# Attention, expert layer and MLP on one core: the first loads in another order, and the value tiles with places of their own in the plan

## The chip, the cores and the metric

The kernel runs on one core of one Trainium2 chip. The metric is the device time of one execution in microseconds (us). The core has a matrix engine (PE, with its weight loads shown as PEld), a vector engine (DVE), a scalar engine (ACT), GpSimd (POOL) and SyncE (SP), which here only issues DMA transfers. Each engine runs its own instructions in order. They meet through semaphores.

## The reference, cut to what matters

```python
# attention: q, k, v (4, 8, 576, 64), s (4, 8, 576)
scores = scale * q @ k.T                       # per batch and head
cum    = cumsum(maximum(s, 0))                 # the "decay sums"
bias   = -(cum[:, :, :, None] - cum[:, :, None, :])
scores = where(causal, -1e9, scores + minimum(bias, 0))
attn   = softmax(scores);  x = attn @ v        # (2304, 512)
# expert layer: each token goes to the best of 8 experts, 512 -> 1024 -> 512
# MLP: 512 -> 2048 -> 512 with h * clip(h + 3, 0, 6) / 6
```

## The kernel before

All products of fp32 data are made of fp16 halves: a number is split into `hi` and `lo`, and three products are summed. The change lies in the attention stage.

Attention has four batches. A batch has five units (128 query rows each, the last one 64), a unit four pairs of heads, so there are 80 pairs. For one pair, PE makes the scores (`S`, L575), DVE adds the decay sums and takes the minimum (`A`, L588), ACT takes the exponential (`E`, L594), PE transposes the result (`T`, L603), ACT and DVE split it (`CD`, L624 and L625), and PE multiplies it with `v` (`V`, L658). A loop over `n` issues step S of pair n+1, A and E of pair n, T and CD of pair n-1, and V of pair n-2; functions put into slot n by `at_slot` or `at_time` follow. `at_time` counts in a plan in which a pair of the five units costs 1.0, 1.5, 2.2, 2.9 and 2.3 (`price`). A scheduler then orders each engine's instructions by a simulated time line, except where `issue_after` ties one instruction behind another.

Four kinds of side work run beside the pairs:

- `load` brings a chunk of 256 rows of q and k (the last chunk has 64). `prep` turns it: POOL lines it up (`xs`), PE transposes (L490), ACT, DVE or POOL split it into `qT` and `kT`.
- `load_v` brings 128 rows of `v` into `v32`, which has two buffers. The `v_part` function makes the halves: ACT writes `hi` (L514), POOL scales (L445) and subtracts (L516). In the kernel before, `v_part` is part of `prep`, and its steps follow the turns of its chunk.
- The decay sums are scanned by DVE for all batches at once (`run`), written to memory (`cum_d`, L407) and read back, repeated over 128 partitions, into the tile `cp` of a batch (`load_cum`, L414). For the first 128 columns of four heads, `first_cum` builds `cp` with PE (L426) and a copy by ACT (L431).
- `fold_cum` copies parts of `cp` for the unit of 64 rows (POOL, L445, 64x576). For the fourth batch these are eight copies into a tile of their own.

From the third batch's fourth unit on, the first expert's weights are loaded (`wf`) and split on POOL (L249, L251, L246) and ACT (L250). POOL also scatters the tokens of a batch (`tok_d`, L804) and gathers rows for the first expert pass (`xg`, L204). Then follow ten expert passes (PE lines L1130 and L1241) and the MLP (L1267 and L1350).

## Time and profile before

| | |
|---|---|
| runs | 875.09, 870.36, 871.22 us; median 871.22 |
| profiled execution | 872.09 us, its span 870.3 us |
| busy over the span | PE 91%, PEld 76%, DVE 72%, ACT 53%, POOL 34% |
| mean granted clock of PE | 0.963 of 2.4 GHz |
| attention stage | from the start to about 275 us |

The span goes from the first to the last instruction of the profiled execution. A row of the chain of waits names what the end of the kernel, followed backwards, waited for at each time; "SPq" is SP's issue of a transfer. In a row of a time line, the brackets at the end give how long the engine was idle before the instruction and what released it.

### The profile page before, as it was taken

Reading aid. Unit: us, or ns where it says so; the run is one execution under the profiler, and the core shown is the slowest. Engines: PE = TensorE matmul, PEld = TensorE weight load, DVE = VectorE, ACT = ScalarE, POOL = GpSimd, SP = SyncE. Lnnn points to the kernel's source line nnn. Section 1 sums busy time; section 2 is a strip of 40 time slices with the busy share of each in tenths; the row PEclk is TensorE's granted clock in tenths of the full one; section 3 lists DMA queues with packets and bytes.
Section 4 is the critical chain, followed back from the end, with each engine's and each line's share of the span. In section 5 each row is a group of like instructions: output and inputs, shape, how many; then the busy total and the mean of one; then the engine's idle time right before and its main releaser. Section 6 shows DMA issues by size and latency. Waiting matters only on the chain.

```text
span 870.3 us, 21871 instructions
## 1 busy us (share of the span) xinstructions
PE 794.4 (91%) x8340; PEld 659.7 (76%) x8340; DVE 623.5 (72%) x1542; ACT 461.7 (53%) x854; POOL 296.4 (34%) x402
## 2 busy tenths in 40 slices
PE   5888788888888998899999999999999999999993
PEld 4567567666667897566778888888888888888882
DVE  4677777866767645789879569988677777777770
ACT  3677767867875433666656343554444344443440
POOL 2565663868984225044331100000022022211232
PEclk8799999999999999999999999999999999999997
DMA  7957245243613678988887355654444545444420
GB/s 165 262 130 214 70 89 180 51 96 101 178 47 79 171 209 219 321 304 273 256 259 270 98 170 165 220 174 158 141 148 129 159 150 162 142 141 153 153 95 27
DMA packets 154327, 142.03 MB, mean 163 GB/s; under 512 B 68710, under 2 KB 122214, under 8 KB 153446
## 3 DMA queue, kind: packets, MB, share of 16 engines
q1 hardware_dynamic: 150422, 130.50, 50.2%
q0 software_dynamic: 3792, 10.06, 3.5%
q8 instruction: 67, 1.10, 0.5%
q14 instruction: 46, 0.38, 0.2%
HBM read 106.70 MB, written 28.54 MB: 155 GB/s over the span
## 4 chain that ended last, share of the span: by engine, by line
PE 48%; DMA 17%; DVE 10%; POOL 7%; ACT 5%; issue 5%; SPq 4%; another core or an unknown queue 1%; POOLq 0%; ACTq 0%; DVEq 0%
PE bank L1350 18%; PE py L1241 8%; PE bank L1267 8%; PE ph L1130 7%; DMA wf<-in_moe_w_dram 5%; DMA v<-in_v_dram 3%; PE pt L603 2%; PE sp L575 2%; PE o L658 2%; DVE wo L1110 2%; DMA t_d<-cl 2%; DMA xsT<-xg 1%; DMA t_d<-sets 1%; ACT pp L594 1%; SPq L215 1%
## 5 line engine op out<-in xcount | busy, mean ns | idle before, releaser
L1267 PE MATMUL bank<-x2T,wi 128*128 128x256 f16 x1728 | 193.5, 273 | 0.9 <-POOL x2T L1249 0.6
L1267 PEld LDWEIGHTS <-wi 128*128 128x128 f16 x1728 | 169.1, 98 | 21.0 <-issue 1.5
L1350 PE MATMUL bank<-wo,sets 128*128 128x256 f16 x1512 | 170.2, 273 | 1.2 <-DVE sets L1279 0.7
L1350 PEld LDWEIGHTS <-sets 128*128 128x128 f16 x1512 | 147.7, 98 | 19.0 <-DVE sets L1279 1.0
L1278 ACT ACTIVATE sets<-back 128x896 f16<-128x896 f32 x72 | 68.1, 950 | 91.9 <-PE bank L1350 74.7
L1130 PE MATMUL ph<-xsT,t 128*128 128x224 f16 (+7 forms) x960 | 109.6, 276 | 3.6 <-DVE hT L1135 3.6
L1241 PE MATMUL py<-hT,t 128*128 128x224 f16 (+7 forms) x960 | 108.4, 273 | 4.2 <-DVE hT L1135 2.3
L1361 POOL TENSOR_TENSOR u<-sa 128x256 f32<-128x256 f32 x9 | 9.3, 1035 | 296.4 <-ACT sa L1360 296.4
L1130 PEld LDWEIGHTS <-t 128*128 128x128 f16 x960 | 86.8, 99 | 24.1 <-issue 4.2
L1241 PEld LDWEIGHTS <-t 128*128 128x128 f16 x960 | 85.5, 98 | 25.7 <-issue 5.7
L1279 DVE SCALAR_TENSOR_TENSOR sets<-back,sets 128x896 f16<-128x896 f32 x72 | 80.2, 1119 | 22.1 <-ACT sets L1278 21.9
L625 DVE SCALAR_TENSOR_TENSOR lo<-pt,hi 128x256 f16<-128x256 f32 (+3 forms) x144 | 72.8, 519 | 28.5 <-ACT hi L624 27.4
L257 DVE SCALAR_TENSOR_TENSOR t<-wf,t 128x1024 f16<-128x1024 f32 x53 | 66.7, 1258 | 28.6 <-ACT t L254 27.9
L658 PE MATMUL o<-v,hi 128*128 128x65 f16 (+2 forms) x960 | 63.0, 201 | 24.9 <-ACT hi L624 17.9
L603 PE MATMUL pt<-idf,pp 128*128 128x128 f32 (+1 forms) x400 | 77.9, 310 | 7.5 <-DVE kT L499 1.9
L624 ACT ACTIVATE hi<-pt 128x256 f16<-128x256 f32 (+3 forms) x144 | 64.1, 460 | 35.4 <-PE pt L603 27.0
L594 ACT ACTIVATE pp<-ne,nm 128x128 f32<-128x128 f32 (+4 forms) x144 | 76.9, 580 | 0.6 <-DVE nm L588 0.6
L254 ACT ACTIVATE t<-wf 128x1024 f16<-128x1024 f32 x53 | 55.5, 1053 | 36.1 <-DMA wf<-in_moe_w_dram 36.1
L588 DVE CUSTOM_DVE_ANT_0 ne<-sp,cp 128x128 f32<-128x128 f32 (+4 forms) x144 | 61.2, 456 | 16.5 <-ACT pp L594 11.4
L658 PEld LDWEIGHTS <-hi 128*128 128x128 f16 (+2 forms) x960 | 47.9, 104 | 32.3 <-ACT hi L624 21.0
L603 PEld LDWEIGHTS pt<-idf,pp 128*128 128x128 f32 (+1 forms) x400 | 46.9, 152 | 17.5 <-issue 3.6
L1249 POOL TENSOR_TENSOR x2T<-y,x2T 128x360 f32 (+5 forms) x24 | 20.8, 871 | 111.1 <-ACT x2T L1248 97.4
(206 smaller groups left out, 1263.4 us busy)
## 6 DMA issues: line engine op xcount, KB each, us to landing
wf<-in_moe_w_dram SPq DMA_DIRECT2D x64, 512.0 KB
back<-t_d SPq DMA_DIRECT2D x144, 128.0 KB
wd<-in_moe_w_in_dram SPq DMA_DIRECT2D x16, 512.0 KB
wd<-in_moe_w_out_dram SPq DMA_DIRECT2D x16, 512.0 KB
cp<-cum_d SPq DMA_DIRECT2D x6, 1152.0 KB
t_d<-cl SPq DMA_DIRECT2D x24, 256.0 KB
t_d<-sets SPq DMA_DIRECT2D x24, 256.0 KB
t_d<-wo SPq DMA_DIRECT2D x24, 256.0 KB
```

The costliest lines, as they stand in the source:

```text
L257: stt(out=lo, in0=fv, scalar=sc, in1=hi, op0=ALU.mult, op1=ALU.subtract)
L594: mark["act"] = nc.scalar.activation(self.view(self.pp, e), self.view(self.ne, e), AF.Exp, bias=self.nm[:, e:e + 1], scale=-1.0).ins
L603: nc.tensor.transpose(self.pt[g][:m, x, :], src, idf)
L624: nc.scalar.activation(hi, pt, AF.Copy, scale=SP)
L625: stt(out=lo, in0=pt, scalar=SP, in1=hi, op0=ALU.mult, op1=ALU.subtract)
L658: mark["pe"] = nc.tensor.matmul(dst, a, x, start=first, stop=last).ins
L1130: mark["pe"] = nc.tensor.matmul(ph[:, :n], wt[c][:, a, cols], xT[:, KD * b_ + c, :n], start=(c == 0 and x == 0), stop=(c == KD - 1 and x = ...
L1241: nc.tensor.matmul(py[:, :rows], wt2[:, j_, f, cols], hT[i_][:, f, :rows], start=(f == 0 and x == 0), stop=(f == KF - 1 and x == 2),)
L1267: m = nc.tensor.matmul(dst, wi[:, a, kk, fs], x2[:, KD * b_ + kk], start=(kk == 0 and x == 0), stop=(kk == KD - 1 and x == 2),)
L1278: nc.scalar.activation(hi, t, AF.Copy, scale=SG)
L1279: stt(out=lo, in0=t, scalar=SG, in1=hi, op0=ALU.mult, op1=ALU.subtract)
L1350: m = nc.tensor.matmul(banks[k_][:, :HM], sets[:, s % 4, a, k_], w_sums[f][:, b_, k_], start=(f == 0 and x == 0), stop=(f == HO - 1 and x ...
```

## The change

The change does four things.

1. On SP's queue the first tile of `v` (batch 0, rows 0 to 127) and the second chunk of q and k are now issued right after the first chunk, ahead of everything that depends on the decay sums. `cum_d` is written from ACT's queue instead of SP's. `first_cum` builds the first 128 columns for all eight heads, in two steps of four, and one load brings columns 128 to 255.
2. `v_part` is taken out of `prep`. Each tile of `v` gets a time of its own, and its load is put 3.0 plan units ahead of it. For the fourth batch the times come from `v_last`. The copy by ACT is tied behind the last exponential issued so far.
3. The load of a later batch's `cp` is tied behind the write of `x_d` issued last (`late_cum`).
4. The fourth batch's eight copies of sums are tied behind the last `hi16` on POOL.

```diff
-        with tc.issue_after(ahead[0]):
-            cum_out = nc.sync.dma_start(cum_d, cum_sb)
+        last = [ahead[0]]
+        def then(f, *args):
+            with tc.issue_after(last[0]):
+                last[0] = f(*args).ins
+        then(load_v, 0, 0)
+        then(load, 0, 1)
+        nc.scalar.dma_start(cum_d, cum_sb)
...
-        def first_cum():
+        def first_cum(h0):
...
-            for h in range(FIRST):
+            for h in range(H // 2):
...
-            nc.scalar.activation(cums[0][:, :FIRST, :128], pc, AF.Copy)
+            nc.scalar.activation(cums[0][:, h0:h0 + H // 2, :128], pc, AF.Copy)
...
-                    hi16(both[b][rows, 2 * p], cums[b][rows, 2 * p + e])
+                    with tc.issue_after(mark["gp"]) if b + 1 == B else ExitStack():
+                        hi16(both[b][rows, 2 * p], cums[b][rows, 2 * p + e])
...
+        def v_part(b, j):
+            def f():
+                m = R[j]
+                v32 = loaded.pop((b, j, "v"))
+                vt = vbuf[b % 2][j]
+                with tc.issue_after(mark["act"]):
+                    nc.scalar.activation(vt[:m, :, 0:D], v32[:m], AF.Copy, scale=SV)
+                hi16(v32[:m], v32[:m], SV)
+                gtt(out=vt[:m, :, D + 1:], in0=v32[:m], in1=vt[:m, :, 0:D], op=ALU.subtract)
+            return f
...
-        then(load_cum, 0, slice(FIRST, H), 0, 256)
-        then(load_cum, 0, slice(0, FIRST), 128, 256)
-        then(load_v, 0, 0)
-        then(load, 0, 1)
+        then(load_cum, 0, slice(0, H), 128, 256)
         then(load_v, 0, 1)
...
+        v_last = (4.5, 6.5, 22.0, 24.0, 26.0)
...
+                if b + 1 == B:
+                    tv = start_of(NCH * (b - 1)) + v_last[j]
+                elif c == 2:
+                    tv = start_of(NCH * b) + 8.5
+                else:
+                    tv = t0 + (nt + x) * per
+                at_time(tv - 3.0, lambda b=b, j=j: load_v(b, j))
+                at_time(tv, lambda j=j, hold=hold: hold[j]())
...
+                    def late_cum(b=b, x=x):
+                        with tc.issue_after(mark["x"]):
+                            load_cum(b, slice(H // 2 * x, H // 2 * x + H // 2))
```

How instructions move is shown at three places. A name such as `v_0_185` is a tile and a running number; lines of the changed kernel have their own numbers. The first place is SP's queue right after the eight transfers of the first chunk of q and k. Before:

```order
L407 DMA cum_d<-cum_sb 32x576
L414 DMA cp<-cum_d 128x4x256
L414 DMA cp<-cum_d 128x4x128
L341 DMA v_219<-in_v_dram 64x8x64 x2
L329 DMA k_223<-in_k_dram 128x8x128
L329 DMA q_222<-in_q_dram 128x8x128
L341 DMA v_226<-in_v_dram 64x8x64 x2
L897 DMA wgf_101<-in_moe_w_gate_dram 128x4x8
L897 DMA wgf_102<-in_moe_w_gate_dram 64x2x8 x4
L414 DMA cp<-cum_d 128x8x320
L341 DMA v_235<-in_v_dram 64x8x64 x2
L414 DMA cp<-cum_d 128x2304 x2
```

The same stretch of SP's queue in the changed kernel, where L421 is the read of the sums:

```order
L341 DMA v_215<-in_v_dram 64x8x64 x2
L329 DMA k_219<-in_k_dram 128x8x128
L329 DMA q_218<-in_q_dram 128x8x128
L421 DMA cp<-cum_d 128x8x128
L341 DMA v_225<-in_v_dram 64x8x64 x2
L410 DMA wgf_101<-in_moe_w_gate_dram 128x4x8
L410 DMA wgf_102<-in_moe_w_gate_dram 64x2x8 x4
L421 DMA cp<-cum_d 128x8x320
L341 DMA v_234<-in_v_dram 64x8x64 x2
L341 DMA v_237<-in_v_dram 64x8x64 x2
```

The write of `cum_d` has left the queue, `v` and the second chunk stand ahead of the first read of the sums, and the two large reads of the second batch's sums (128x2304) have left the stretch. The second place is ACT in the first unit. Before, where `v_0_185` and `v_1_187` are the first two tiles of `v`:

```order
L594 ACTIVATE pp<-ne,nm 128x128 x4
L624 ACTIVATE hi<-pt 128x256
L594 ACTIVATE pp<-ne,nm 128x128
L514 ACTIVATE v_0_185<-v_219 128x8x64
L594 ACTIVATE pp<-ne,nm 128x128
L514 ACTIVATE v_1_187<-v_226 128x8x64
L498 ACTIVATE kT<-pk 128x2x256
L624 ACTIVATE hi<-pt 128x256
L594 ACTIVATE pp<-ne,nm 128x128 x2
```

ACT in the first unit of the changed kernel (L601 is the exponential, L459 the copy of `v`, L515 a turned chunk, L520 a turned q):

```order
L601 ACTIVATE pp<-ne,nm 128x128 x4
L459 ACTIVATE v_0_185<-v_215 128x8x64
L515 ACTIVATE qT<-pk 128x512
L515 ACTIVATE kT<-pk 128x2x256
L631 ACTIVATE hi<-pt 128x256 x2
L601 ACTIVATE pp<-ne,nm 128x128 x2
L459 ACTIVATE v_1_187<-v_225 128x8x64
L601 ACTIVATE pp<-ne,nm 128x128
L520 ACTIVATE xs<-pk 128x512
L601 ACTIVATE pp<-ne,nm 128x128
```

The copy of the first `v` moves ahead by one split and one exponential, that of the second `v` keeps its place ahead of the last exponentials of the unit, and the second chunk's `kT` moves ahead of two splits. The third place is POOL around the third batch's fourth unit, from the scatter of the second batch's tokens on. Before:

```order
L804 DMA tok_d<-what,pos_s 5120x3 x5
L445 TENSOR_SCALAR cp<-cp 64x576 x3
L249 TENSOR_SCALAR wf<-wf 128x1024
L251 TENSOR_TENSOR t_3949<-wf,t_3949 128x1024
L688 TENSOR_TENSOR xw<-xr,xw 128x512
```

The same stretch of POOL in the changed kernel, where `v_3696` and `v_3699` are tiles of the fourth batch's `v`:

```order
L811 DMA tok_d<-what,pos_s 5120x3 x5
L451 TENSOR_SCALAR cp<-cp 64x576 x2
L451 TENSOR_SCALAR v_3696<-v_3696 128x512
L451 TENSOR_SCALAR cp<-cp 64x576
L451 TENSOR_SCALAR v_3699<-v_3699 128x512
L461 TENSOR_TENSOR v_2_199<-v_3696,v_2_199 128x8x64
L461 TENSOR_TENSOR v_3_201<-v_3699,v_3_201 128x8x64
L249 TENSOR_SCALAR wf<-wf 128x1024
```

Two of the fourth batch's value tiles now stand between the scatter and the first split of the expert's weights; a third follows a few rows later. In the kernel before, all five of them come ahead of this scatter.

## Rows read from the trace of the kernel before

**Rows 1.** Chain of waits, 7 to 32 us (start us, us, what)
```profile
7.80 1.65 DMA cum_d<-cum_sb
...
12.56 3.14 SPq L329
...
15.75 1.43 SPq L341
...
24.07 7.26 DMA v<-in_v_dram
```

**Rows 2.** Who waited for whom, 0 to 60 us (us in total, times, longest)
```profile
ACT v L514 <- DMA v<-in_v_dram: 14.8, 6, 4.3
```

**Rows 3.** Time line of ACT (start us, us, line, operation, out<-in, idle before)
```profile
11.76 0.69 ACT L594 ACTIVATE pp<-ne,nm 128x128 f32<-128x128 f32 x2 [0.19 <-DVE nm L588]
...
17.60 0.64 ACT L514 ACTIVATE v<-v 128x512 f16<-128x512 f32 x1 [3.35 <-DMA v<-in_v_dram]
...
39.68 1.11 ACT L594 ACTIVATE pp<-ne,nm 128x384 f32<-128x384 f32 x2
...
81.06 0.68 ACT L594 ACTIVATE pp<-ne,nm 128x128 f32<-128x128 f32 x2
...
98.40 0.64 ACT L514 ACTIVATE v<-v 128x512 f16<-128x512 f32 x1 [4.24 <-DMA v<-in_v_dram]
...
102.53 1.14 ACT L594 ACTIVATE pp<-ne,nm 128x384 f32<-128x384 f32 x2
...
119.98 0.49 ACT L624 ACTIVATE hi<-pt 128x384 f16<-128x384 f32 x1 [3.93 <-remote]
...
145.24 0.68 ACT L594 ACTIVATE pp<-ne,nm 128x128 f32<-128x128 f32 x2
...
160.48 0.64 ACT L514 ACTIVATE v<-v 128x512 f16<-128x512 f32 x1 [1.84 <-DMA v<-in_v_dram]
```

**Rows 4.** Stretches: busy us of each engine, PE clock, DMA share, GB/s
```profile
14.00:20.00 6.00, 1.79 (x22) 1.16 (x23) 1.58 (x11) 1.17 (x3) 1.36 (x3) 0.56 1.14 251
...
200.00:220.00 20.00, 16.06 (x268) 12.21 (x266) 12.88 (x51) 16.27 (x36) 19.47 (x21) 0.91 0.30 83
220.00:240.00 20.00, 17.18 (x235) 12.67 (x230) 14.76 (x62) 17.56 (x39) 18.88 (x23) 0.91 0.57 175
...
520.00:600.00 80.00, 80.00 (x735) 71.71 (x734) 68.35 (x142) 37.89 (x64) 0.00 (x0) 1.00 0.55 183
```

**Rows 5.** Time line of PE and ACT, 5 to 9 us: `first_cum`
```profile
5.59 2.07 PE L426 MATMUL pf<-run,idf 32*128 32x128 f32 x8
...
7.70 0.60 ACT L431 ACTIVATE cp<-pf 128x512 f32<-128x512 f32 x1
```

**Rows 6.** Page, DMA issues: the reads of the sums
```profile
cp<-cum_d SPq DMA_DIRECT2D x6, 1152.0 KB
```

**Rows 7.** Time line of POOL, 164 to 257 us
```profile
164.79 0.62 POOL L445 TENSOR_SCALAR v<-v 128x512 f32<-128x512 f32 x1
165.49 1.13 POOL L516 TENSOR_TENSOR v<-v,v 128x512 f16<-128x512 f32 x1
...
185.01 1.94 POOL L445 TENSOR_SCALAR cp<-cp 64x576 f32<-64x576 f32 x3 [4.35 <-DVE nm L588]
...
205.77 5.79 POOL L445 TENSOR_SCALAR cp<-cp 64x576 f32<-64x576 f32 x8
...
250.75 2.15 POOL L246 TENSOR_TENSOR t<-wf,t 128x1024 f16<-128x1024 f32 x1
...
256.78 1.02 POOL L204 DMA_INDIRECT xg<-x_d,slots  x1 [1.51 <-issue]
```

**Rows 8.** Time line of SP: the last transpose for expert pass 0
```profile
262.32 1.26 SPq L215 DMA_TRANSPOSE xsT<-xg  x1
```

**Rows 9.** Chain of waits at the first expert product
```profile
275.45 2.30 PE ph L1130 x24
```

More of the change, by code (lines that the diff above doesn't have):

```diff
@@ L414, in load_cum @@
             return nc.sync.dma_start(cums[b][:, hs, a:z], rows.partition_broadcast(128)[:, 0])
[L416 to L418 removed]
+        def first_cum(h0):
             if 0 not in cums:
                 cums[0] = a2.tile([128, H, S], F32, tag="cp", name="cp")
[L424 to L425 removed]
+            pc = psT.tile([128, H // 2, 128], F32, tag="T", name="pf")
+            for h in range(H // 2):
                 nc.tensor.matmul(
[L427 removed]
+                    pc[:, h], idf[:BH, h0 + h:h0 + h + 1].to_broadcast([BH, 128]),
                     run[:, :128].rearrange("h (p r) -> h r p", r=2),
@@ L507, in turn @@
                 return [line_up, flip]
-            def v_part(j):
-                def f():
-                    m = R[j]
-                    v32 = loaded.pop((b, j, "v"))
-                    vt = vbuf[b % 2][j]
-                    nc.scalar.activation(vt[:m, :, 0:D], v32[:m], AF.Copy, scale=SV)
-                    hi16(v32[:m], v32[:m], SV)
-                    gtt(out=vt[:m, :, D + 1:], in0=v32[:m], in1=vt[:m, :, 0:D], op=ALU.subtract)
-                return f
-            vs = [v_part(t0 // 128 + j) for j in range(nr)]
+            vs = [v_part(b, t0 // 128 + j) for j in range(nr)]
             groups = ((0, 1), (2, 3)) if big else (range(NP),)
@@ L889, in start_of @@
             return begins[NP * place[u] + p]
-        last = [cum_out.ins]
-        def then(f, *args):
-            with tc.issue_after(last[0]):
-                last[0] = f(*args).ins
-        then(load_cum, 0, slice(FIRST, H), 0, 256)
-        then(load_cum, 0, slice(0, FIRST), 128, 256)
-        then(load_v, 0, 0)
-        then(load, 0, 1)
+        then(load_cum, 0, slice(0, H), 128, 256)
         then(load_v, 0, 1)
@@ L909 @@
         then(load, 0, 2)
-        at_slot(-1, first_cum)
+        for h0 in (0, H // 2):
+            at_slot(-1, lambda h0=h0: first_cum(h0))
         for x, fs in enumerate(prep(0, 0, fast=True)):
@@ L934, in begin @@
                 hold["f"] = prep(b, c)
+            hold.update((j, v_part(b, j)) for j in range(NCH))
             def next_load(g=g):
@@ L940 @@
             at_time(t0, begin)
-            for j in range(CH[c][0] // 128, CH[c][0] // 128 + (2 if c < 2 else 1)):
-                at_time(t0, lambda b=b, j=j: load_v(b, j))
+            nt = 4 if c < 2 else 2
+            for x, j in enumerate(range(CH[c][0] // 128, CH[c][0] // 128 + (2 if c < 2 else 1))):
+                if b + 1 == B:
[6 more added lines that the diff above has]
+                at_time(tv, lambda j=j, hold=hold: hold[j]())
             at_time(t0, next_load)
-            for x in range(6 if c < 2 else 3):
-                for y in range(2 if x < (4 if c < 2 else 2) else 1):
+            for x in range(nt):
+                for y in range(2):
                     at_time(t0 + (x + 1.3 * y) * per, lambda x=x, y=y, hold=hold: hold["f"][x][y]())
```

7 lines of the change are left out of this document (2 added, 5 removed).

## The prediction, made before the changed kernel was run

> **What bounds the kernel now.** I read the stretches first, then the chain of waits, then who waited for whom, then the time lines of ACT and POOL. The stretches [rows 4] split the kernel in two. From the MLP on, PE is busy all the time (80.00 of 80.00 us), and the number and order of PE's instructions there do not change, so that part can only start earlier or later. The first expert product starts at 275.45 us [rows 9]; what the change is worth is how far that moves. In attention no engine is full for long: it is a chain of small steps, in which a wait of one engine is soon a wait of all.
>
> The chain of waits [rows 1] shows who waits at the start. It goes through the write of the sums, then through SP's issue of the second chunk (3.14 us) and of the second `v` (1.43 us), and then through the landing of the third `v` (7.26 us). The list of waits gives the other end: ACT waited 14.8 us for tiles of `v` in the first 60 us [rows 2]. ACT runs in order, so exponentials that were ready stood behind these copies.
>
> The time line of ACT [rows 3] gives the pace without such waits. Units 0 and 1 take 39.68 - 11.76 = 27.9 us in the first batch; in the second they take 102.53 - 81.06 = 21.5 us, of which 4.24 are a wait for `v`, so 17.2 us of work, 2.15 us a pair. Units 2 to 4 take 81.06 - 39.68 = 41.4 us in the first batch; in the second 145.24 - 102.53 = 42.7 us, of which 3.93 are a wait whose cause the profile does not show, so 38.8 us.
>
> **The change, part by part.** All sums are against the profiled execution, 872.09 us (its span of 870.3 and 1.8 around it), which is 0.87 above the median of the runs.
>
> 1. *The first two units.* Added are four more L426 and one more copy. The four that are there took PE 2.07 us, the copy 0.60 us on ACT [rows 5]. PE goes straight on to the next transposes, so I put 2.1 us on the path; the copy runs beside them. The first exponential comes at 11.8 + 2.1 = 13.9 us. Does the data come in time? In the new order of SP's queue stand one `v` (128x512 fp32, 0.26 MB), the second chunk (1.05), `cp` for 128 columns (0.52), one `v` (0.26), `cp` for 320 columns (1.31) and two `v` (0.52). At 251 GB/s [rows 4], from about 8 us, when the first write of the sums could go [rows 1], with 1.65 us from the same row for the landing: the second chunk is there at 14.9 us, the first `cp` at 17.0, the second `v` at 18.0, the fourth `v` at 25.3. At 2.15 us a pair ACT asks for the second chunk (some 2 us of POOL and PE later) at about 18.2, for the second `v` at 20.3, for that `cp` at 22.5, for the fourth `v` at 26.8. Each is just in time, with 1.2 us to spare at the least. At full pace unit 2 would start at 13.9 + 17.2 = 31.1 us; I take 32, since the margins are thin: **7.7 us** gained. The ends are 8.6 (full pace) and 1.3 (only the first wait, 3.35 us [rows 3], goes, and the 2.07 are paid). I take a value near the upper end because the two large reads of the second batch's sums, 2.36 MB [rows 6] or 9.4 us at that rate, also leave this stretch.
>
> 2. *Units 2 to 4 of the first batch.* Free of waits they would gain 41.4 - 38.8 = 2.6 us. ACT now copies two tiles of the second batch's `v` there, which the second batch's own stretch did not have: 2 x 0.64 [rows 3]. I take **1.3 us**. The ends are 2.6 and a loss of 2: the fifth `v` stands behind the next batch's first chunk, 1.05 MB or 4.2 us, with about one pair to spare.
>
> 3. *Second batch.* The wait of 4.24 us goes, since the load is put 3.0 plan units ahead of its copy: **4.2 us**, between 0 and 4.2. The tile next behind on ACT is a split that PE has ready.
>
> 4. *Third batch.* In the same way 1.84 us [rows 3]: **1.8 us**, between 0 and 1.8.
>
> 5. *From the third batch's fourth unit on.* Three tiles of the fourth batch's `v` now fall here, each 0.62 and 1.13 us on POOL [rows 7], 5.2 us in all. POOL stood idle for 4.35 us at that place [rows 7], which hides most of it; 0.9 is left. The read of the fourth batch's `cp`, 9.4 us of transfer, is tied behind a row write of this batch and so moves toward the first loads of the expert's weights, on which POOL waits next. From 200 to 240 us POOL is busy 19.47 and 18.88 of 20 us [rows 4], so what is late there stays late. The ends are 0 and 5.2 + 9.4 = 14.6; I take **2.5 us lost**, near the lower end, because the read is issued about a unit ahead of the weights.
>
> 6. *The eight copies of sums.* 5.79 us on POOL [rows 7], the same number before and after; other POOL work goes ahead of them. With POOL full on either side I count nothing; the ends are 5.8 either way.
>
> 7. *The gather for the first expert pass.* Two splits of the expert's weights (L246, 2.15 us each [rows 7]) now stand ahead of the scatter of tokens, so `xg` comes 4.3 us later than its place. Its transposes were issued by 262.32 + 1.26 = 263.6 us [rows 8], PE needed them at 275.45 [rows 9]: 11.9 us cover it, and I count nothing; without cover it costs 4.3.
>
> 8. *The write of the sums on ACT's queue.* It landed in 1.65 us with nothing queued behind or beside it [rows 1]. Now 1.31 MB of `v` and second chunk are under way. If it has to wait for all of these, it lands up to 5.2 us later, and every load behind it too; if it goes beside them, nothing. I count nothing and keep 5.2 as the other end. Two rules of the Trainium skill pull apart here. DMA: Bandwidth & Descriptors, section Issuing engines are not separate DMA queues, says that transfers started from several engines run on the same 16 DMA engines and that only issue time is saved; by that alone the write would be as late as rival A has it, and the time its time. The same page, Queues, rings and completion order, says that each DMA engine takes packets in turn from the rings that have work; by that a write of 72 KB gets through early, and the sum stays. No row of the kernel before shows two such queues at once.
>
> Sum: -7.7 - 1.3 - 4.2 - 1.8 + 2.5 = **-12.5 us**, 859.6 us for a profiled execution, 858.7 for the median: **859 us**. The rows say what is late next: in the first unit the second chunk and then the fourth `v`; in the last third POOL.
>
> **The rivals.**
>
> *A: the write of the sums waits for the loads ahead.* For it: it shares the DMA engines with 1.31 MB, at a share of 1.14 in such a stretch [rows 4]. Against it: it is on another queue. DVE then waits for `cp` in unit 1. Part 1 shrinks to 2.5 us: 872.1 - 7.3 = 864.8, 864 as a median.
>
> *B: the change does not do what it says after the first batch.* `v32` keeps two buffers, so a load still waits until POOL has read the tile two back, however early it stands. For it: POOL had other work between. Against it: the tiles are now spread out. Parts 3 and 4 vanish: -6.5, 865.6, 865 as a median. Both A and B: -1.3, 870.
>
> *C, slower: POOL's queue becomes the bound of the last third.* The place is the fourth unit of the third batch, the price 5.2 us of `v`, 9.4 us of waiting for the expert's weights behind the read of `cp`, and 5.8 us of copies that then stand in front of a row write: 20.4 us against gains of 15.0. It decides from the point where POOL's idle 4.35 us are used up and the first weights have not landed. For it: POOL is full from 200 to 240 us. Against it: POOL's work in sum is unchanged, and the loads are a unit apart. 872.1 + 5.4 = 877.5, 877 as a median.
>
> *D: more than forecast.* Full pace in parts 1 and 2, nothing lost in 5, and the copies of part 6 hidden: -8.6 - 2.6 - 6.0 - 5.8 = -23, 848.
>
> **How the numbers follow.** The forecast has 0.56, with a range of its own of 853 to 863; A 0.12, B 0.10, D 0.08, A with B 0.07, C 0.07. Faster by over 0.5% (4.4 us, about what a measurement of this kernel can tell from no change): forecast, A, B and D, 0.86. Within 0.5%: A with B, 0.07. Slower: C, 0.07. For 8 in 10 the range goes from 850, which leaves out most of D, to 868, which takes in A and B and leaves out C and most of A with B.
>
> **What would show it.** Right: no wait of ACT for `v` over 1 us in the first 60 us; first exponential at about 13.9 us, unit 2 at about 32, second batch's first at about 72 instead of 81.06, third's at about 132 instead of 145.24; the first expert product at about 263. Wrong in part 1: unit 2 later than 35 us, with DVE waiting for `cp` (A) or ACT for the fourth `v`. Wrong in 3 and 4: the waits for `v` are still there (B). Wrong in 5: POOL waits for `wf` for several us, and the last batch takes longer than the others. The forecast is wrong as a whole if the second batch starts no earlier than 78 us.

## The result, and the profile after

The changed kernel took 883.01 us (median of four runs, 882.22 to 885.46), the kernel before 870.79 beside it. The ratio is 1.0139 [1.0095, 1.0182]: slower, and outside the predicted range. The profiled execution, the slowest of the four, took 885.46 us, 13.4 more than that of before. In a later series (E12 below) the changed kernel took 881.95 against 873.35, 1.0098 [1.0064, 1.0132].

In the changed kernel the lines of attention have higher numbers: L594 became L601 (exponential), L445 L451 and L516 L461 (POOL), L514 L459 (ACT's copy of `v`), L414 L421 (read of the sums), L804 L811 (scatter). Expert layer and MLP lie 16 lines later.

The head of the page, with the span, then busy time, share and count by engine:

```profile
span 883.8 us, 21892 instructions
PE 804.5 (91%) x8348; PEld 666.4 (75%) x8348; DVE 621.8 (70%) x1542; ACT 462.1 (52%) x855; POOL 296.7 (34%) x402
```

Shares nearly as before: nothing here says where 13 us went. The time line of ACT does, at the same places as [rows 3]:

```profile
13.30 0.98 ACT L601 ACTIVATE pp<-ne,nm 128x128 f32<-128x128 f32 x3 [0.96 <-DVE nm L595]
...
35.52 0.60 ACT L601 ACTIVATE pp<-ne,nm 128x384 f32<-128x384 f32 x1
...
73.53 0.68 ACT L601 ACTIVATE pp<-ne,nm 128x128 f32<-128x128 f32 x2
...
133.91 0.68 ACT L601 ACTIVATE pp<-ne,nm 128x128 f32<-128x128 f32 x2
...
187.04 0.64 ACT L459 ACTIVATE v<-v 64x512 f16<-64x512 f32 x1 [9.56 <-DMA v<-in_v_dram]
...
205.97 0.68 ACT L601 ACTIVATE pp<-ne,nm 128x128 f32<-128x128 f32 x2
```

The second batch starts at 73.53 instead of 81.06, the third at 133.91 instead of 145.24: 11.3 us gained. The fourth starts at 205.97 instead of 210.21, so 7.1 us were given back within the third batch. There ACT stood 9.56 us before a copy of `v`: the kind of wait that the change took away at the start stands here again.

The rest of the way, as first exponential of a batch, last exponential, first expert product, first MLP product, and last MLP product of the first kind, all in us:

| | batch 2 | 3 | 4 | last exp. | experts | MLP starts | MLP length | span |
|---|---|---|---|---|---|---|---|---|
| before | 81.06 | 145.24 | 210.21 | 268.87 | 275.3 | 498.7 | 332.1 | 870.3 |
| after | 73.53 | 133.91 | 205.97 | 267.23 | 277.8 | 506.0 | 339.1 | 883.8 |
| after, later series | 72.25 | 132.55 | 202.54 | 267.05 | 275.8 | 498.5 | 339.7 | 877.8 |

(MLP length runs from its first to its last product of L1283, before L1267. "Last exp." is the middle of the row of the last two exponentials.) Two findings are the same in both profiles of the changed kernel: all 11 to 13 us of gain are lost again before the experts start, and the MLP takes 7.0 to 7.6 us longer. The expert passes, from the first expert product to the start of the MLP, were 4.8 us longer in the first of the two profiles only.

The MLP. PE, DVE, ACT and POOL by stretch (columns as in [rows 4]), after:

```profile
520.00:600.00 80.00, 77.62 (x705) 68.46 (x703) 62.61 (x132) 35.41 (x59) 0.00 (x0) 1.00 0.56 179
...
546.00:666.00 120.00, 114.45 (x1033) 100.60 (x1032) 91.10 (x179) 54.02 (x88) 5.99 (x6) 1.00 0.49 161
```

and the same 120 us of the MLP before:

```profile
539.00:659.00 120.00, 119.74 (x1098) 107.18 (x1097) 94.86 (x187) 55.96 (x90) 5.99 (x6) 1.00 0.50 167
```

PE was full before (80.00 of 80.00 in the first of these stretches [rows 4]) and now stands 5.55 us of 120, at the full granted clock (1.00) both times. So the loss is in waits, not in the clock. The time lines of ACT, DVE and PE after show one such wait:

```profile
557.06 0.68 ACT L1074 ACTIVATE m<-wd 128x512 f32<-128x512 f32 x1 [4.13 <-DMA wd<-in_moe_w_out_dram]
559.76 0.66 ACT L1074 ACTIVATE m<-wd 128x512 f32<-128x512 f32 x1 [2.03 <-DMA wd<-in_moe_w_out_dram]
560.64 0.67 ACT L1290 ACTIVATE wo<-bank,three 128x512 f32<-128x512 f32 x1
...
560.77 0.42 DVE L1126 SCALAR_TENSOR_TENSOR wo<-m,wo 128x256 f16<-128x256 f32 x1 [5.29 <-ACT wo L1125]
...
562.38 0.68 DVE L1291 SCALAR_TENSOR_TENSOR wo<-wo,bank 128x512 f32<-128x512 f32 x1
...
563.11 3.11 PE L1283 MATMUL bank<-x2T,wi 128*128 128x256 f16 x27 [0.96 <-DVE wo L1291]
```

ACT's read of a PSUM bank (PSUM holds PE's results; L1290) stands behind two conversions of weights that wait for their loads (4.13 and 2.03 us). DVE has waited 5.29 us for ACT and frees the bank late, and PE stands. Before, ACT's read of the bank into `wo` stood ahead of both conversions, and these waited 2.46 and 0.68 us:

```profile
547.09 0.68 ACT L1058 ACTIVATE m<-wd 128x512 f32<-128x512 f32 x1 [2.46 <-DMA wd<-in_moe_w_out_dram]
...
549.07 0.68 ACT L1058 ACTIVATE m<-wd 128x512 f32<-128x512 f32 x1 [0.68 <-DMA wd<-in_moe_w_out_dram]
550.16 0.69 ACT L1274 ACTIVATE cl<-bank,three 128x512 f32<-128x512 f32 x1 [0.42 <-DMA t_d<-cl]
```

The list of waits of PE over the whole length of the MLP has more than this one, after (line, what it waited for, us in total, times, longest):

```profile
PE bank L1366 <- DVE wo L1291: 2.3, 1, 2.3
PE bank L1283 <- DVE wo L1291: 2.0, 3, 1.0
PE bank L1283 <- DVE cl L1291: 0.8, 2, 0.6
PE bank L1283 <- DVE sets L1291: 0.5, 2, 0.2
```

and before:

```profile
PE bank L1267 <- DVE wo L1275: 0.3, 1, 0.3
```

So PE waits 5.6 us for DVE instead of 0.3. The longest wait, 2.3 us, is of another kind: no conversion of weights stands just ahead of it. DVE waits 3.19 us for ACT, and ACT waits until the last contents of the tile `wo` have been stored to memory (`t_d`):

```profile
630.70 0.69 ACT L1290 ACTIVATE wo<-bank,three 128x512 f32<-128x512 f32 x1 [3.56 <-DMA t_d<-wo]
```

Nothing in the change touches the MLP. But the scheduler orders each engine by a simulated time line, and that line has moved. PE's rows in the MLP are the same; those of ACT, DVE and SP are not. At the first of these places, ACT's queue (`m<-wd` waits for a load, `bank` rows free PE's banks), before on the left:

```
cl<-bank,three           cl<-bank,three
sets<-bank,three         sets<-bank,three
wo<-bank,three           m<-wd
m<-wd                    m<-wd
wo<-m                    wo<-m
wo<-m                    wo<-bank,three
m<-wd                    wo<-m
```

The read `wo<-bank` has changed sides with the weights.

The third batch. POOL, after, where [rows 7] showed 4.35 us of idle time that a row of DVE (L588) ended:

```profile
170.17 0.93 POOL L811 DMA_INDIRECT tok_d<-what,pos_s  x1 [0.31 <-issue]
179.52 1.31 POOL L451 TENSOR_SCALAR cp<-cp 64x576 f32<-64x576 f32 x2 [8.42 <-DMA tok_d<-what,pos_s]
180.91 0.62 POOL L451 TENSOR_SCALAR v<-v 128x512 f32<-128x512 f32 x1
...
182.94 2.21 POOL L461 TENSOR_TENSOR v<-v,v 128x512 f16<-128x512 f32 x2
```

and SP's queue, with the load that ACT waited for:

```profile
163.75 0.94 SPq L421 DMA_DIRECT2D cp<-cum_d  x2
...
169.45 1.16 SPq L239 DMA_DIRECT2D wf<-in_moe_w_dram  x1
184.10 0.61 SPq L343 DMA_DIRECT2D v<-in_v_dram  x1
```

POOL's copy of sums waits for the five scatters of tokens to land. The read of the next sums, 2.36 MB, now starts at 163.75, just ahead of them (139.0 before), and the idle time is 8.42 us instead of 4.35. Behind it stand two splits of batch four's `v`. Only when the first is done (184.1) is one of the two `v32` buffers free and the last `v` tile loaded; ACT meets it at 187.04. The fourth unit of the third batch takes 25.6 us instead of 20.7. The first two tiles of that `v` lie in the second unit, and from 134 to 165 us the list of waits has a wait of ACT of the same kind, 3.8 us in one (1.84 before [rows 3]):

```profile
ACT v L459 <- DMA v<-in_v_dram: 3.8, 1, 3.8
```

POOL and the end of attention, by stretch:

```profile
200.00:220.00 20.00, 17.87 (x280) 13.79 (x282) 13.36 (x57) 14.85 (x36) 15.91 (x16) 0.91 0.41 119
220.00:240.00 20.00, 17.68 (x220) 12.24 (x217) 13.77 (x52) 15.60 (x34) 16.69 (x23) 0.83 0.46 153
```

POOL was busy 19.47 and 18.88 us there before [rows 4]: it has become less busy, not fuller.

### The profile page after: what moved, and what is told of

Read it like the earlier page. It is cut to its first block, busy times and chain, and to the rows that moved or that the text cites. A ratio compares the mean times of both kernels' runs of the same rounds, so it can differ in the third digit from the quotient of the medians.

```text
span 883.8 us, 21892 instructions
## 1 busy us (share of the span) xinstructions
PE 804.5 (91%) x8348; PEld 666.4 (75%) x8348; DVE 621.8 (70%) x1542; ACT 462.1 (52%) x855; POOL 296.7 (34%) x402
## 5 line engine op out<-in xcount | busy, mean ns | idle before, releaser
L1283 PE MATMUL bank<-x2T,wi 128*128 128x256 f16 x1728 | 195.1, 273 | 3.9 <-DVE wo L1291 2.0
L1283 PEld LDWEIGHTS <-wi 128*128 128x128 f16 x1728 | 168.6, 98 | 25.9 <-issue 5.5
L1366 PE MATMUL bank<-wo,sets 128*128 128x256 f16 x1512 | 170.3, 273 | 3.3 <-DVE wo L1291 2.3
L1366 PEld LDWEIGHTS <-sets 128*128 128x128 f16 x1512 | 147.3, 98 | 21.9 <-issue 2.6
L1257 PE MATMUL py<-hT,t 128*128 128x224 f16 (+7 forms) x960 | 111.6, 279 | 3.9 <-DVE hT L1151 3.1
L1257 PEld LDWEIGHTS <-t 128*128 128x128 f16 x960 | 87.9, 100 | 26.2 <-issue 5.0
L1146 PEld LDWEIGHTS <-t 128*128 128x128 f16 x960 | 86.9, 99 | 25.7 <-issue 5.6
L610 PE MATMUL pt<-idf,pp 128*128 128x128 f32 (+1 forms) x400 | 77.8, 312 | 13.4 <-ACT xs L520 8.7
L632 DVE SCALAR_TENSOR_TENSOR lo<-pt,hi 128x256 f16<-128x256 f32 (+3 forms) x144 | 72.0, 518 | 21.7 <-ACT hi L631 21.1
L601 ACT ACTIVATE pp<-ne,nm 128x128 f32<-128x128 f32 (+4 forms) x144 | 76.8, 579 | 1.6 <-DVE nm L595 1.6
L595 DVE CUSTOM_DVE_ANT_0 ne<-sp,cp 128x128 f32<-128x128 f32 (+4 forms) x144 | 61.1, 455 | 18.1 <-ACT pp L601 7.5
L1354 DVE TENSOR_TENSOR back<-back 128x256 f32<-128x256 f32 x72 | 33.9, 471 | 38.5 <-DMA back<-t_d 34.5
```

The costliest lines, as they stand in the source:

```text
L601: mark["act"] = nc.scalar.activation(self.view(self.pp, e), self.view(self.ne, e), AF.Exp, bias=self.nm[:, e:e + 1], scale=-1.0).ins
L610: nc.tensor.transpose(self.pt[g][:m, x, :], src, idf)
L632: stt(out=lo, in0=pt, scalar=SP, in1=hi, op0=ALU.mult, op1=ALU.subtract)
L1146: mark["pe"] = nc.tensor.matmul(ph[:, :n], wt[c][:, a, cols], xT[:, KD * b_ + c, :n], start=(c == 0 and x == 0), stop=(c == KD - 1 and x = ...
L1257: nc.tensor.matmul(py[:, :rows], wt2[:, j_, f, cols], hT[i_][:, f, :rows], start=(f == 0 and x == 0), stop=(f == KF - 1 and x == 2),)
L1283: m = nc.tensor.matmul(dst, wi[:, a, kk, fs], x2[:, KD * b_ + kk], start=(kk == 0 and x == 0), stop=(kk == KD - 1 and x == 2),)
```

## The experiments

Four theories stood. *Collision*: the tied read of the sums makes the scatters land late, and POOL stands. *Tiles*: batch four's `v`, put into the third batch, makes ACT and POOL wait there. *Copies*: the tied copies of sums hold POOL back. *Order*: the MLP is longer because the scheduler's order of ACT and DVE differs there, whatever the cause. Times are medians; ratios stand against before in the same series. "Fourth unit" is that of the third batch, "batch four" runs from its first to its last exponential, all in us. The columns of times come from one profile of each kernel and are good to 0.1 us; the ratio is an estimate from all runs with its 95% interval, not the quotient of the medians. E1 to E4, E5 to E8, E9 to E12 and E13 to E16 were measured in four series, in which before took 873.07, 869.31, 873.35 and 870.35 us, so medians compare only within a series.

| | batch 3 starts | fourth unit | batch four | experts | MLP length | median | ratio |
|---|---|---|---|---|---|---|---|
| before | 145.24 | 20.7 | 58.7 | 275.3 | 332.1 | | |
| after | 133.91 | 25.6 | 61.3 | 277.8 | 339.1 | 883.01 | 1.0139 [1.0095, 1.0182] |
| E1 first loads alone | 137.72 | 20.7 | 59.0 | 268.7 | 331.7 | 868.49 | 0.9960 [0.9931, 0.9989] |
| E2 sums read early | 137.04 | 24.7 | 62.4 | 274.8 | 334.2 | 873.87 | 1.0012 [0.9981, 1.0042] |
| E3 read tie alone | 147.73 | 21.3 | 74.5 | 295.7 | 332.6 | 889.36 | 1.0169 [1.0127, 1.0211] |
| E4 copies not tied | 134.63 | 23.1 | 76.6 | 289.0 | 331.7 | 885.0 | 1.0132 [1.0089, 1.0174] |
| E5 neither tied | 135.42 | 24.0 | 66.2 | 276.4 | 336.3 | 869.54 | 0.9995 [0.9972, 1.0019] |
| E6 `v` of batches 2, 3 | 131.39 | 22.4 | 75.6 | 283.2 | 341.1 | 886.92 | 1.0205 [1.0162, 1.0247] |
| E7 first loads, copies | 136.72 | 21.9 | 58.7 | 266.8 | 331.7 | 864.30 | 0.9951 [0.9928, 0.9975] |
| E8 last `v` by rule | 132.29 | 20.7 | 70.0 | 272.0 | 332.1 | 868.42 | 0.9979 [0.9956, 1.0002] |
| E9 last `v` one earlier | 134.27 | 25.2 | 61.0 | 274.3 | 334.3 | 873.72 | 0.9990 [0.9962, 1.0018] |
| E10 as E8, read early | 137.17 | 21.7 | 64.5 | 277.0 | 334.5 | 877.31 | 1.0059 [1.0032, 1.0087] |
| E11 as E8, two reads tied | 133.34 | 22.3 | 65.3 | 275.4 | 334.2 | 872.57 | 0.9985 [0.9959, 1.0011] |
| E12 after, again | 132.55 | 24.6 | 64.5 | 275.8 | 339.7 | 881.95 | 1.0098 [1.0064, 1.0132] |
| E13 as E8, splits behind | 130.23 | 20.7 | 55.8 | 263.3 | 336.5 | 867.71 | 0.9971 [0.9945, 0.9996] |
| E14 after, splits behind | 131.03 | 24.9 | 65.3 | 274.2 | 338.6 | 876.25 | 1.0098 [1.0060, 1.0137] |
| E15 as E11, splits behind | 131.5 | 22.2 | 57.8 | 263.6 | 333.5 | 868.43 | 0.9976 [0.9954, 0.9998] |
| E16 as E7, splits behind | 136.44 | 21.7 | 61.1 | 273.9 | 336.4 | 875.3 | 1.0040 [1.0015, 1.0065] |

**E1, first loads alone.** Before, with part 1 of the change only:

```diff
+        then(load_v, 0, 0)
+        then(load, 0, 1)
+        nc.scalar.dma_start(cum_d, cum_sb)
...
+        for h0 in (0, H // 2):
+            at_slot(-1, lambda h0=h0: first_cum(h0))
```

> Only the first part of the change, on the kernel before: first v and second chunk ahead of the sums, the write of the sums on ACT's queue, the first sums of all eight heads by PE. Theory 1 (the early part works as forecast, the loss comes later in the change): unit 2 near 35.5 us, second batch's first exponential near 74 instead of 81.06, first expert product near 268 to 270, time 863 to 866. Rival (an early gain in attention is given back before the experts in any case): second batch near 74, but first expert product at 273 to 277, time 869 to 873.

The experts start 6.6 us earlier, and the profiled span is 7.8 us shorter (862.5). But that execution was the fastest of twelve; by all runs the gain is 0.4%, some 3.5 us, and the median of 868.49 lies above the forecast. So steps 1 and 2 of the prediction gain on their own, but only about half of it is seen at the end.

**E2, sums read early.** The changed kernel without the tie of the reads:

```diff
-                        with tc.issue_after(mark["x"]):
-                            load_cum(b, slice(H // 2 * x, H // 2 * x + H // 2))
+                        load_cum(b, slice(H // 2 * x, H // 2 * x + H // 2))
```

> The changed kernel without the tie of the reads of the next batch's sums behind a row write, so they are issued at their plan time again, tens of us ahead of the scatter of tokens. Theory 1 (read and scatter on top of each other make the scatter land in 8.4 us instead of some 4, POOL's next copy waits for that landing, and in the third batch a v load and ACT wait behind POOL): the waits of 8.42 fall to some 4, ACT's wait of 9.56 for v goes, fourth batch starts near 196 instead of 205.97, first expert product near 268, time 871 to 875 (the order in the MLP changes again, by an unknown amount of some us). Rival 2 (the stall of the third batch is POOL's work on the three v tiles of batch four): ACT's wait for v stays above 6 us, fourth batch at 204 to 206, time 881 to 885.

The wait for the scatters shrinks, as collision says:

```profile
177.83 1.31 POOL L451 TENSOR_SCALAR cp<-cp 64x576 f32<-64x576 f32 x2 [5.46 <-DMA tok_d<-what,pos_s]
```

and ACT's wait for the last `v` falls from 9.56 us to 1.08:

```profile
186.20 0.64 ACT L459 ACTIVATE v<-v 64x512 f16<-64x512 f32 x1 [1.08 <-DMA v<-in_v_dram]
```

but the fourth unit stays at 24.7. Neither collision nor this one wait of ACT is what makes it long. The ratio nevertheless falls to 1.0012: of the 11.8 us between the two spans (872.0 and 883.8), 3.0 lie ahead of the experts, 4.4 in the passes and 4.9 in the MLP.

**E3, read tie alone.** Before, with the tie that E2 removed.

> The kernel before with that tie alone. Theory 1: the scatters of the second and third batch land in 8 us instead of 4, POOL waits for each, 4 to 5 us lost twice at most, fourth batch's first exponential at 214 to 220 instead of 210.21, time 875 to 880. Rival 2 (v tiles): no loss, 869 to 873.

The wait for the scatters is there, on its own and as long as in the changed kernel:

```profile
191.94 1.94 POOL L445 TENSOR_SCALAR cp<-cp 64x576 f32<-64x576 f32 x3 [9.05 <-DMA tok_d<-what,pos_s]
```

The fourth unit takes only 0.6 us more for it. The price comes a batch later: batch four takes 74.5 us instead of 58.7.

**E4, copies not tied**, and **E5, neither tied.** The changed kernel without the tie of the eight copies, and without both ties.

```diff
-                    with tc.issue_after(mark["gp"]) if b + 1 == B else ExitStack():
-                        hi16(both[b][rows, 2 * p], cums[b][rows, 2 * p + e])
+                    hi16(both[b][rows, 2 * p], cums[b][rows, 2 * p + e])
```

> The changed kernel without the tie that puts the eight copies of batch four's sums behind other work on POOL. In this kernel the instructions of VectorE, ScalarE and SyncE in the MLP stand in the order of the kernel before again. Theory 3 (of the loss some 6 us is MLP time, from the order of VectorE there: from the first hidden product of the MLP to the end 371.6 us before, 377.8 after): MLP back to 371 to 372, the stall at 176 to 190 us is still there, time 875 to 879. Rival (the MLP's length goes with something else, the transfers or the clock, not with the order): MLP stays at 376 to 378, time 881 to 885.

> The changed kernel without both ties (reads of the sums at their plan time, copies of batch four's sums where the kernel before has them); the first part and all new places for v stay. The MLP's instructions stand nearly as in the kernel before. Theory now (the stall of the third batch comes from batch four's v tiles, since it stayed with the reads early; the read's tie costs in batch four): third batch's unit 5 still long, 23 to 25 us instead of 20.7, batch four 63 to 68 us, first expert product at 272 to 276, MLP 332 us, profiled span 868 to 873. Rival (the copies' tie is needed, since new v places push the copies into the way): batch four 72 us or more, first expert product over 282, span 877 or more.

E4's batch four is 15 us longer than that of the changed kernel, so the copies' tie helps, given the read's tie. Its MLP is back at 331.7 though the experts start 11 us later: a late start is not what makes the MLP long.

**E6, `v` of batches 2 and 3.** First loads and the new places of `v` for the second and third batch; no ties, and the fourth batch by the same rule as the others.

> The first part, and the new v places for batches two and three alone: no ties, and batch four's v by the same rule as theirs. The MLP's instructions on ScalarE and SyncE stand in the changed kernel's order. Theory: no stall in the third batch (unit 5 20.5 to 21.5 us), first expert product at 265 to 270; but the MLP takes 338 to 340 us from its first to its last hidden product, as in the changed kernel, against 332 before, because of that order: span 866 to 871. Rival (the MLP's length does not hang on the order): 332 us, span 859 to 864.

The third batch starts earlier than in any kernel with `v` in its old place, and then batch four takes 75.6 and the MLP 341.1. The gain is real and is given back, as in the changed kernel.

**E7, first loads and the copies' tie.** E1 and the tie that E4 removed.

> The first part of the change and the tie of batch four's eight copies, nothing else. Theory (that tie pays only where the read of the sums comes late): first expert product within 2 us of that of the first part alone (268.7), span 860 to 865. Rival (the tie is worth some 11 us by itself, as between the changed kernel and the one without it): first expert product at 257 to 262, span 851 to 856.

The lowest ratio of all, 864.30 us against 869.31, though its interval overlaps those of E1, E13 and E15. The copies' tie brings the experts 1.9 us forward against E1, as the theory says.

**E8, last `v` by rule.** The changed kernel without `v_last`; batch four's `v` is placed like that of the others.

```diff
-                if b + 1 == B:
-                    tv = start_of(NCH * (b - 1)) + v_last[j]
-                elif c == 2:
+                if c == 2:
```

> The changed kernel with batch four's v by the rule of the other batches; both ties stay. The MLP's instructions stand in the order of the kernel before. Theory (batch four's v tiles make the stall): unit 5 of the third batch 20.5 to 22 us instead of 25.6, first expert product at 270 to 275, MLP 332 us, span 866 to 872. Rival (the read of the sums on top of the scatter makes the stall): unit 5 stays at 24 us or more, first expert product 276 or later, span 873 or more.

ACT now copies batch four's `v` at 171.0, 180.9, 195.2, 200.7 and 210.5 us (143.5, 150.7, 170.7, 171.2 and 187.0 in the changed kernel), without a wait for a load. The fourth unit is back at 20.7 with both ties in place, and the three units ahead of it take 27.2 us (31.3 in the changed kernel, 29.7 before): the places of the tiles cost the third batch 9.0 us up to there, 7.3 by E12's profile. The same edit takes the fourth unit from 24.7 (E2) to 21.7 (E10) with the reads early, and from 24.9 (E14) to 20.7 (E13) with the splits behind the scatter, so tiles is shown; by which waits they act is not, since those differ from run to run. With these few lines out the ratio falls from 1.0139 to 0.9979. The MLP is back at 332.1, and PE is full again in it:

```profile
534.00:654.00 120.00, 120.00 (x1102) 107.55 (x1100) 94.70 (x184) 55.91 (x90) 5.98 (x6) 1.00 0.49 165
```

But batch four takes 70.0. The time lines of POOL, PE and ACT show how:

```profile
235.67 2.12 POOL L246 TENSOR_TENSOR t<-wf,t 128x1024 f16<-128x1024 f32 x1
...
238.56 2.14 POOL L246 TENSOR_TENSOR t<-wf,t 128x1024 f16<-128x1024 f32 x1
...
243.99 1.09 POOL L811 DMA_INDIRECT tok_d<-what,pos_s  x1 [0.25 <-POOL acc L821]
...
250.17 0.23 POOL L821 TENSOR_TENSOR acc<-acc,oh 64x8 f16<-64x8 f16 x1
250.45 0.17 PE L790 MATMUL pr<-acc,ones 128*128 128x8 f16 x1 [5.42 <-POOL acc L821]
251.71 0.75 ACT L631 ACTIVATE hi<-pt 128x512 f16<-128x512 f32 x2 [7.05 <-PE pt L610]
```

The splits of the expert's weights stand ahead of the routing of tokens on POOL; PE has a small routing product in its queue (L790), waits 5.42 us for it, and ACT then 7.05 for PE.

**E9, last `v` one earlier**, and **E12, the changed kernel again**, in one series.

```diff
-        v_last = (4.5, 6.5, 22.0, 24.0, 26.0)
+        v_last = (4.5, 6.5, 21.0, 23.0, 25.0)
```

> The changed kernel with the last three v tiles of batch four one plan unit earlier (21, 23, 25 instead of 22, 24, 26); nothing else. This is enough to give the MLP another order on VectorE and ScalarE, that of the kernel with the reads early, whose MLP took 334.2 us from its first to its last hidden product. Theory (the MLP's length is the order's): third batch's stall stays (unit 5 24 to 26 us), MLP 332 to 335 us instead of 339.1, span 876 to 880. Rival (the order does not matter): MLP 338 us or more, span 881 to 886.

> The changed kernel once more, for a second profile of it. If what its first profile showed is the kernel's own: unit 5 of the third batch 25 to 26 us, first expert product at 277 to 279, the passes from there to the first hidden product of the MLP 228 us (5 more than in every other kernel), MLP 339. If the 5 us in the passes belong to that one execution: passes 222 to 224, and span 878 to 880.

One plan unit is worth 8.2 us of median. The fourth unit stays long (25.2 and 24.6), attention ends within 1.5 us of the same time, but the MLP takes 334.3 and 339.7. PE over 120 us of it, E9, then E12, and PE's wait for DVE in E9's whole MLP:

```profile
542.00:662.00 120.00, 117.76 (x1078) 105.20 (x1076) 93.98 (x182) 54.84 (x89) 5.97 (x6) 1.00 0.50 165
```

```profile
538.00:658.00 120.00, 114.74 (x1036) 101.06 (x1035) 91.38 (x180) 53.86 (x87) 5.97 (x6) 1.00 0.48 160
```

```profile
PE bank L1366 <- DVE wo L1291: 2.1, 1, 2.1
```

The waits ahead of L1283 are gone in E9 (3.3 us in the first profile of the changed kernel, 2.1 in E12); the long one ahead of L1366 stays.

**E10 and E11, fewer tied reads.** E8 with no read tied (there the third load of `v` of a batch is put at 7.5 plan units instead of 8.5 as well), and with all but the fourth batch's reads tied.

> The first part, the v places of batches two and three (the third of a batch's loads at 7.5 plan units instead of 8.5), batch four's v by the same rule, the copies' tie; the reads of the sums at their plan time. The MLP stands in the order of the kernel before. Theory: no stall in the third batch, batch four starts at 199 to 202 us and takes 59 to 62, first expert product at 264 to 268, MLP 332, span 856 to 860, faster than the first part with the copies' tie (858.9). Rival (batch four starts earlier only to wait for POOL and the weights there): first expert product at 270 to 275, span 862 to 867.

> The changed kernel with batch four's v by the rule of the others, and the reads' tie for batches two and three alone: batch four's read at its plan time. MLP in the order of the kernel before. Theory (batch four's read on top of the third batch's scatter is what lengthens batch four from 59 to 70 us): batch four starts at 195 to 198, takes 59 to 63, first expert product at 262 to 266, span 854 to 859. Rival (batch four is held by POOL's order of weights and routing, not by the read): it takes 67 us or more, first expert product at 270 or later, span 863 or more.

Neither brings batch four under 64 us, so the reads alone do not explain it.

**E13 to E16, splits behind the scatter.** In E8, the changed kernel, E11 and E7, three of POOL's splits of expert weights are tied behind the scatter of batch four's tokens issued last, and are put five slots later:

```diff
+                    with tc.issue_after(mark["pool"]):
+                        gtt(out=lo, in0=fv, in1=hi, op=ALU.subtract)
...
-            at_slot(n + 3, lambda x=x: splits[x]())
+            at_slot(n + (8 if x >= KD + KF // 2 else 3), lambda x=x: splits[x]())
```

> The kernel with batch four's v by rule (both ties), and POOL's last three splits of expert weights (L246) tied behind batch four's scatter. MLP in the order of the kernel before. Theory (these splits ahead of the routing hold PE, and with it batch four): batch four takes 59 to 63 us instead of 70, first expert product at 261 to 266 instead of 272.0, span 854 to 859. Rival (batch four is held by the weights' arrival or the late read): it takes 67 us or more, first expert product at 270 or later, span 863 or more.

> The changed kernel with the same tie of the three splits and nothing else; the MLP's order is a third one that no run has had. Theory: batch four 57 to 59 us instead of 61.3 to 64.5, and the first expert product 6.5 us after the last exponential instead of 8.8 to 10.6, so at 268 to 272 instead of 275.8 to 277.8; span 866 to 876 by the MLP's order. Rival: first expert product at 275 or later.

> The kernel with two reads tied (batch four's read at its plan time), with the same tie of the splits. MLP in the order of the kernel before. Theory: batch four 59 to 61 us instead of 65.3, first expert product at 267 to 270 instead of 275.4, span 858 to 862. Rival: 65 us, 274 or later, span 868 or more.

> The fastest so far (first part and copies' tie) with the same tie of the splits; there one split stands ahead of the scatter, two behind. The MLP's order becomes another. Theory: batch four 57.5 to 59 us against 58.7, first expert product at 265 to 267 against 266.8, MLP 332 to 336, span 857 to 863: no gain to speak of. Rival (the splits cost 2 us each wherever they stand): first expert product at 262 or earlier.

In E13 batch four falls from 70.0 to 55.8, in E15 from 65.3 to 57.8. For these two the cause is shown: weight splits ahead of the routing. The scatter of E13, and its gather for the experts:

```profile
237.44 1.11 POOL L812 DMA_INDIRECT tok_d<-what,pos_s  x1 [0.54 <-POOL pos_s L807]
...
249.91 1.01 POOL L204 DMA_INDIRECT xg<-x_d,slots  x1 [6.30 <-DMA slots<-tok_d]
```

The end gained nothing by it (0.9971 against E8's 0.9979): the three splits now stand from 257.8 to 264.2 us, where the experts start (263.3). The experts start only 8.7 us earlier though batch four is 14.2 us shorter, the passes take 228.3 us instead of 222.3, and the MLP begins 2.7 us earlier and takes 4.4 longer. In it PE waits 2.9 us once, where ACT again waits for a store:

```profile
612.13 0.69 ACT L1289 ACTIVATE wo<-bank,three 128x512 f32<-128x512 f32 x1 [4.51 <-DMA t_d<-wo]
```

In the changed kernel itself (E14) the same edit left batch four at 65.3; there ACT waited for another step of the routing:

```profile
254.05 0.21 ACT L799 ACTIVATE what<-ix 128x2 f32<-128x2 f32 x1 [5.62 <-POOL ix L763]
```

and to the fastest kernel it did harm (1.0040). So that it is these splits in the changed kernel too is not shown.

Several forecasts of these runs missed clearly: the time of E3 (889, forecast 875 to 880), E6 (experts at 283.2, forecast 265 to 270), E10 (span 874.2, forecast 856 to 860), E13 (span 867.0, forecast 854 to 859) and E16 (span 876.6, forecast 857 to 863).

## Why the prediction was wrong

**Steps 1 to 3 were right in sum, not in their parts.** The first exponential came at 13.30 (13.9 was forecast), the second batch at 73.53 (72), the third at 133.91 (132): 11.3 us of 13.2, and 12.7 in E12. But the third unit of the first batch came at 35.52, not 32, past the 35 that the prediction itself set as a sign of error in step 1: that step gave 4.2 us of 7.7 (5.7 in E12). Step 2 gave 3.4 instead of 1.3, and step 3 gave 3.8 of 4.2. Rival A fell: no wait of DVE for a read of the sums is in the list. In the first 60 us ACT waited once for `v` (3.5 us, where none over 1 us was forecast and 14.8 had been [rows 2]).

```profile
ACT v L459 <- DMA v<-in_v_dram: 3.5, 1, 3.5
```

**Rival B** did not come true for the second batch, where no wait of ACT for `v` is left. But its mechanism is the one that held batch four's tiles in the third batch: a load waits until POOL has read the tile two back, however early it stands. POOL's subtractions ended at 144.50 and 184.05 us, and the loads that ACT then waited for started at 144.53 (its second half at 147.72, behind two writes of `x_d`) and 184.10. The 3.0 plan units of lead do not help there.

**Step 8 was between its two ends.** For the write of the sums on ACT's queue the list by tile shows (start, then time to landing):

```profile
L414 ACTq DMA_DIRECT2D cum_d<-cum_sb x1: 360/360/360, 7.8 to 7.8; - x1
...
DMA to landing us min/median/max: 4.2/4.2/4.2
```

4.2 us instead of 1.65: 2.6 of the 5.2 us that rival A had. It cost nothing that can be seen, since PE builds the first columns. The two rules of the Trainium skill (DMA: Bandwidth & Descriptors, sections Issuing engines are not separate DMA queues, and Queues, rings and completion order) were put against each other as wholly late or not late at all. They do not pull apart: the first section also says that such transfers interleave. The trace agrees with that: the write landed at 12.05 us, ahead of the load of q on SP's queue that was issued just before it (7.74, landed at 13.62), and later than alone.

**Step 4 failed in the changed kernel.** 1.8 us of gain were forecast up to the third batch's fourth unit, since ACT's wait of 1.84 us for `v` was to go. A wait of that kind is still there, 3.8 us long and ahead of the second tile of batch four's `v`, and the changed kernel lost 1.6 us up to there (0.9 in E12). With these tiles later (E8) no such wait is left, and 29.7 - 27.2 = 2.5 us are gained.

**Step 5 failed, and cost most in attention.** "POOL stood idle for 4.35 us at that place, which hides most of it." That idle time was a wait in POOL's queue (ended by a row of DVE before, by the last scatter's landing after), and what is queued behind it runs later, not inside it. Two of the three tiles stood behind that wait, and the load of the third behind them. E8 moves the tiles and the fourth unit is back at 20.7 (25.6). ACT's wait for that load is only part of the path: it was 9.56 us in the first profile, 4.23 in E12 and 1.08 in E2, and the unit took 25.6, 24.6 and 24.7. The read of the sums did lengthen the wait (E2, E3), but cost 0.6 us in this unit where no tiles stood behind it (E3). From the fourth unit to the experts 2.5 us of loss were forecast and 12.4 measured: 4.9 in the fourth unit, 0.7 in the fifth, 2.6 in batch four, 4.2 behind it. In the later series batch four lost 5.8.

**Step 7's cover was half gone.** The gather and the transposes behind it, after:

```profile
265.11 1.08 POOL L204 DMA_INDIRECT xg<-x_d,slots  x1 [5.65 <-PE pt L610]
```

```profile
270.65 1.27 SPq L215 DMA_TRANSPOSE xsT<-xg  x1
```

The last transposes were issued by 271.9 and the first product ran at 277.8: 5.9 us, where 11.9 had been. The cover itself still held.

**The premise on the MLP failed, and was the largest single term.** "The number and order of PE's instructions there do not change, so that part can only start earlier or later." PE's order was the same, and the MLP took 7.0 us more (7.6 in E12): PE waited 5.6 us (5.8 in E12) for DVE to free banks, where it had waited 0.3. The prediction looked at PE's order alone; the order of ACT, DVE and SP had changed.

The runs fall into groups by that order, taken from the tiles of the rows, whatever the time of start. With the order of before eleven kernels, that of before among them, take 331.7 to 336.5; with that of the changed kernel three (two profiles of it, and E6) take 339.1 to 341.1; E2 and E9 share a third order and take 334.2 and 334.3; E14 and E16 have orders of their own (338.6, 336.4). E9 against E12 comes nearest to a test: the experts start within 1.5 us of each other, and the MLP differs by 5.4. What the order adds is seen in PE's waits ahead of L1283: 3.3 us in the changed kernel (2.1 in E12), 0.3 before, none in E9. The orders of the three engines changed together, so which of them does it is not shown.

The order does not explain the long wait ahead of L1366 (2.3 us, and 2.9 in E12). Kernels with the order of before have it too: 2.46 us in E5, 2.27 in E10, 2.18 in E11, 2.87 in E13. The kernel before, E1, E4, E7 and E8 have no wait over 0.30 us at that place. It is more than half of what parts the eleven. What makes the store late that ACT waits for there is open.

**Rival C** named the right third of attention and came closest, 877 us, at a chance of 0.07. That was luck: its mechanism was wrong, since POOL did not fill up but waited, and it had no term for the MLP.

In sum, for the later series: attention -12.7 up to the third batch and +13.2 behind it, MLP +7.6, and the passes -0.7, 7.5 us of span. Open is which single row holds batch four up in the changed kernel, and what makes the passes longer in some profiles: they take 227.4 to 228.3 us in five (the first of the changed kernel, E9, E13, E15, E16) and 221.5 to 223.8 in all others, E12 among them. In the first of the five the granted clock was 0.87 and 0.88 of full speed from 320 to 360 us (0.91 and 1.00 before).

## What to carry to other kernels

An idle stretch in an in-order queue hides new work only if the new work stands ahead of the waiting instruction; look up what the idle time waits for before counting it as cover. Where a scheduler orders a whole program, an edit in one stage can reorder all later ones: compare every engine's order in the later stages, not only the busiest one's, above all where reads that free PSUM banks share a queue with work that waits for loads or stores. A buffer that is free only when a slow engine has read it sets when the next load starts, however early the load is put. And a time gained early is worth only what the last stages let through; here the first loads, with the copies' tie or without it, gave more than the whole change.

## What the runs showed of the hardware

- With a 2.36 MB read started just ahead of five scatters, POOL's copy waited 8.42 us for the last of them to land (behind 171 us in the changed kernel), and 9.05 in E3. With the read tens of us earlier it waited 5.46 (E2), and 3.95 in the kernel before, behind 119 us.
- A 72 KB write on ACT's queue, issued at 7.8 us into loads of 1.31 MB on SP's, landed in 4.2 us; on SP's own queue, with no load issued behind it yet, it took 1.65 [rows 1].
- With the same PE instructions in the same order, the MLP took between 331.7 and 341.1 us; at the full granted clock PE lost 5.55 us of 120 in the changed kernel, most of it in waits for DVE to free PSUM banks (2.3 us the longest).
